# A new order of issue and new engines for the 2587 steps of a fused masked attention and Mish FFN

## The chip, the cores and the metric

The kernel runs on one core of one Trainium2 chip. The time is device microseconds (us) of one execution. TensorE (PE), VectorE (DVE), ScalarE (ACT), GpSimd (POOL) and SyncE (SP, here only an issuer of DMAs) each work through a queue of their own in order; the kernel fixes by hand what stands in each queue, and semaphores tie the queues together.

## The reference

The inputs are q, k and v of shape (4, 8, 768, 64), a projection of 64x6, and two weights of 512x2048 and 2048x512, all float32.

```python
q_bucket = sum((einsum('bhsd,dk->bhsk', q, proj) > 0) * 2**arange(6))   # likewise k_bucket
mask   = q_bucket[:, :, :, None] == k_bucket[:, :, None, :]
scores = where(mask, scale * q @ k.T, -1e9)
attn   = exp(scores - max(scores)); attn = attn / (sum(attn) + 1e-9)
x = (attn @ v).transpose(0, 2, 1, 3).reshape(3072, 512)
h = x @ w_in
g = h * tanh(log1p(exp(h)))          # Mish; for h > 20 the inner function is h itself
out = g @ w_out
```

## The kernel before, in words

Every operand of a product is split into two float16 halves (a high part and the rest), and a product is three float16 matmuls; only the first stretch uses float32 matmuls, because there the halves are not ready.

The work is cut into 12 units (4 batches of 3 units, a unit is 256 query rows of all 8 heads). A unit has 8 score slots of the attention and 8 pieces of the FFN; the FFN of a unit runs three blocks behind its attention. There are 96 score slots in all. The steps of one score slot n, with the lines that a trace shows, are:

- S: the scores on PE into three PSUM banks (L941, or L952 in float32 for the first units), with the bucket bits as a second half of the contraction, so that a masked score is lower by a large constant.
- max on DVE (L982), the reduction over two heads at once; then mb, three tiny operations that make scale and bias of the exponential. It can run on DVE in one piece or column by column (L965 with L969 or L972) or on POOL (L976 and L977).
- exp on ACT (L995, once for each head), which reads the PSUM banks and writes `pb`. From slot 8 on all scores share one PSUM tile (`ps_s`), so S of slot n+1 waits for exp of slot n.
- In unit 0 the exponentials are turned by PE (tp, L424) and copied out of PSUM by ACT (L427) or DVE (L428). In later units they are scaled by the reciprocal of their sum and split: hi (L380 on POOL, L382 on ACT, L383 on DVE) and lo (L398 on DVE, or L404 and L405 on POOL), and a DMA transpose issued by SP turns them (L462, `PT<-hl`).
- V: the product with v on PE (L1092; L1066 in float32 in unit 0, with a spread of the reciprocals, L1076, ahead of it).

The FFN pieces are H (L1120, L1130 to L1132) on PE, Mish on ACT (L1151), a split of the result as above (`ffb`), and O (L1169, L1179 to L1181) on PE, then a copy (L1222 on ACT, L1228 on DVE) and a store (L1232). Exponential and Mish are in two table sets of ACT; the kernel writes a table load (L1340) wherever the next step of ACT needs the other set.

Ahead of the first slots stand the preparation of q and k: float32 turns on PE (L440), a hash on PE (L451) and its threshold on DVE (L454), sums of squares on ACT (L470), a sum over partitions on PE (L488, L489) whose exponent DVE takes (L493, L475), the projection's halves (L513, L514), and for later slots the f16 halves of k (k_hi L383/L380, k_lo L398 or L404 and L405) that SP turns into `KT` (L462, `KT<-wo`). The weights are loaded by SP (L458), unpacked (L586 on ACT, L589 or L593, L599) and split during the first units. Several tiles serve as storage for something else at first: `KT<-wo` is a turn of the halves of k that lie in `wo`, and `stg<-in_moe_w_in` a load of half a piece of w_in into `stg`.

What sets the order is a table. The kernel first only lists its 2587 steps; a step has one to four ways to be done, each on an engine, and `ORDER` is a string of step numbers, each with a letter for the way ("a" is left out). This loop writes the instructions in that order, and each engine meets its own in that order:

```python
for w in ORDER.split():
    n, a = (int(w[:-1]), "abcd".index(w[-1])) if w[-1].isalpha() else (int(w), 0)
    o = self.ops[n]
    assert all(q in done for q in o.preds), o.name
    done.add(o)
    if o.kind and o.kind != table:
        table = o.kind
        load(table)
    yield o.alts[a][2]
```

The ways of mb, as an example of a step with four:

```python
op("mb", [("DVE", 300, lambda: scale(both, False)), ("DVE", 400, lambda: scale(each, False)),
          ("DVE", 500, lambda: scale(each, True)), ("POOL", 600, scale_pool)], ...)
```

Of the kernel before, what the change touches and what calls it, by code (L numbers as in the profile page):

```python
# [86 lines left out]
7 9 0 50 20 22 19 11 12 1 2 3 4 76 29 80 5 77 52 30 13 37 60 25 81b 6 17 26b 38 10 14 15 18 33 34 48 54 57 56 21  # L87
53 39b 63 27 61 35 62 28 31 36 32 78 64 65 16 79 86 82 87 88c 8 137 40 41b 147 83 117 92 94b 138 42 51 43 44 89
109 110b 153 111 90 66 154 112 67 118 119c 120 132 113 115 114 116 124 133 125b 155 126 121 148 46b 91 93b 139b
140b 122 156 107b 123 45 127b 149 134d 23 58 24 59 95 101 135 136 141 55 47 178 96 128 97 99 98 142 84 143 129  # L90
68 100 174 176 175 177 69 170 130 179 171b 168d 108 180 131 172 70 71 204 182 173b 157 189 205b 144b 158 159c
190b 181 193 145b 102 198 191 185 192 186 220 187 206 194 150 199b 85 103 221 161b 195d 160c 197 188 307 222d
258 207 196 216 218 217b 219b 183d 104 223 146 49 152 162 151 106 105 212 213b 163 214 243 210b 215b 184 164 169
211 224 248 239 241 240 353 242 270 235 236 254 255 237 256 244 245b 238 246 233d 249 166b 354 247 262 271 250
200 257 234 259 263b 272d 165b 355 208 251 273 225 292 266 268 267 269 283 293 294 284 349 226 368 357b 350 264
265b 303 285 304b 227 209 305 295 296 201 260d 309d 310 167 356c 306 312b 252 253 203 232 202 291 311c 274 228
281b 261 282 322 286b 317 318 319b 364 287 365 289 288 290 366 313b 323c 308 324 321 320 367 72 330b 369b 231
358 338 315 331 275 325 297 332 276b 298b 229 339 340d 334 230 341 342 397 314 73 333b 74 299 399 336 277 370b
# [12 lines left out]
687 636b 665b 668 639 640c 641 689 619b 680 715b 624 653 716 625b 670c 717 661b 726 679 626 681 727 728d 719 690
720 730 729 718 683 682 732d 691 692c 782 694 662 666 733 721 669 734b 695 778 723 724 741 736 742 775 779 776b
791 696 697 743 792 744 745 765c 735b 693b 672 698 699b 671 777b 766 738 722 737 725 731 795 773 700 637 739 767
768c 769 770 780b 771 772 702 781b 796 703 786 740 704 814 787 815 829 788d 793b 790 789 806d 705 797c 673 706c
708 794 807 808 809 816 817 818 784 810 819 820 799 830 747 709 746 837 811 812 813 821b 822 823c 783 798b 800
801 707 748 749 832 831 710 833 711 713 834c 849 858 750 825b 835 836 826 824c 827 751 712b 752c 754 850 851 761
874 714 828 861 881 762 877 862 863 875 864 852b 854 865 866d 885 853c 763 856 867 868c 870 755 878 756 890 886
855 857 871 882 753 838 894 879 869b 757 880 887c 839 872 785 759 888 889 910 911 883 884 859b 764 895 901c 891
902 903 912 913b 914 905 915 916c 873 909 898 758b 840 842b 760 899 896b 841 892b 904c 1053 907 917 918c 927 900
928 929c 920b 897 956 1174 843 908 906 1012 921 844 960 931 930 933c 942 845 919c 893b 846 922 934 847b 848 935b  # L120
804 802 943 944b 937 924 957 970 926 925 1013 945 958b 946 947c 964 936c 803 939 948 923 938 860 971 949c 1014
1015b 961 950 951 965 940 952 941 932 974 955 966 962 967d 953 1016c 1052 959 1054 969 968 981c 975 982 983 1017
991 992 993 990 805b 985 994 995 996c 954 1018 978 986 876 979 984b 987 963 988 1007 997 972c 973b 980 1008 1009
998 1000 976b 1010 1011 1025c 977 999c 1026 1002b 989 1055 1005 1001 1028 1003 1036 1019 1004 1059 1024 1037
1038 1027c 1029 1039 1040 1041c 1031 1056 1176 1042 1043c 1063 1045 1064 1065c 1020 1030 1032 1046 1044b 1047
1048 1234 1006 1049 1033 1177 1068 1060 1057b 1061c 1067 1066 1079c 1080 1021b 1058b 1089 1082c 1178 1142 1022
1081b 1083b 1062b 1085b 1072 1069 1090 1091c 1092 1093 1094 1095 1073 1076 1105 1096b 1070c 1077 1050 1179b 1074
1098b 1071b 1034b 1106 1107c 1078 1204 1023 1084 1086 1109 1108 1111d 1097c 1100 1075 1112 1113c 1115b 1138 1088
1134 1120 1139 1135 1087 1152 1103 1121 1122c 1099 1101 1116 1124 1123 1125c 1114c 1181 1117 1126 1127c 1129
1128 1136b 1143 1144 1145c 1110 1102 1148 1133 1131 1147 1146 1118 1137 1159d 1130 1169 1104 1132 1175 1156 1182  # L130
1180c 1160 1161c 1153 1149 1170 1171c 1172 1140 1162b 1141b 1163 1173 1188d 1165 1189 1190c 1192 1199 1119 1164
1193 1166 1200 1168 1167 1157 1205 1206 1207b 1158 1191c 1209 1194 1150c 1154c 1151 1197 1196 1183 1201d 1203
1202 1217c 1218 1220b 1219b 1228 1229 1230c 1231 1221 1232 1248d 1263 1259 1267 1264 1260 1261b 1210 1051 1233
1195 1223 1184 1186 1185 1155 1249 1268 1269b 1270 1250b 1252 1271 1287d 1222 1187 1208c 1251c 1254 1235 1236
# [1236 lines left out]
```

## Time and profile before

| | before |
|---|---|
| time, median of 3 runs | 808.07 us (807.68 to 808.2) |
| profiled execution, its own time | 807.16 us |
| its span | 805.4 us |
| PE busy | 796.2 us, 99% of the span, 6595 instructions |
| DVE busy | 620.0 us, 77% |
| ACT busy | 608.7 us, 76% |
| POOL busy | 383.5 us, 48% |
| DMA | 134.30 MB, mean 167 GB/s |
| instruction queue (q8) | 51 packets, 0.84 MB, 0.4% of the DMA engines' span |
| chain that ended last | PE 97%, DVE 1%, DMA 1% |

Between the span and the profiled execution's own time lie 1.76 us. The profiled execution is 0.91 us below the median of the three runs. In the rows further down, each row of a timeline is one instruction or a run of like ones: start in us from the span's start, length in us, engine, line, operation, tiles written and read; in brackets is how long the engine stood idle just before, and what released it.

### The profile page before, as it was taken

How to read it: one execution, taken by the hardware profiler on the slowest of the kernel's cores; microseconds unless marked ns; L12 is line 12 of the kernel's file. 1: busy time of each engine (PE TensorE's matmuls, PEld its weight loads, DVE VectorE, ACT ScalarE, POOL GpSimd, SP SyncE). 2: the span in 40 equal slices, each digit the busy share in tenths (PEclk: the TensorE clock that was granted, in tenths of full speed). 3: DMA queues.
4: the chain of work that ended last, by engine and by line, in shares of the span. 5: the costliest groups of instructions: out<-in, count | busy, mean ns of one | idle time of the engine just before them, and what ended most of it. 6: DMA issues, size and time to landing. Idle time of an engine off the chain costs nothing.

```text
span 805.4 us, 17073 instructions
## 1 busy us (share of the span) xinstructions
PE 796.2 (99%) x6595; PEld 555.0 (69%) x6595; DVE 620.0 (77%) x1139; ACT 608.7 (76%) x930; POOL 383.5 (48%) x398
## 2 busy tenths in 40 slices
PE   9999999999999999999999999999999999999998
PEld 6566666676786676676676776676676677676676
DVE  4888999997898878889798777887887967657200
ACT  5989998998689687677876787898687585778021
POOL 5565442356274293163534245444664771565040
PEclk9999999999999999999999999999999999999999
DMA  9959999989999886999989988999989658455400
GB/s 293 246 168 245 229 215 182 203 179 211 205 178 188 153 170 135 184 192 213 177 139 178 210 140 152 187 171 212 172 162 160 135 91 153 105 99 113 98 2 26
DMA packets 395490, 134.30 MB, mean 167 GB/s; under 512 B 365456, under 2 KB 386448, under 8 KB 395408
## 3 DMA queue, kind: packets, MB, share of 16 engines
q1 hardware_dynamic: 395408, 133.21, 83.1%
q8 instruction: 51, 0.84, 0.4%
q14 instruction: 31, 0.25, 0.1%
HBM read 35.65 MB, written 6.29 MB: 52 GB/s over the span
## 4 chain that ended last, share of the span: by engine, by line
PE 97%; DVE 1%; DMA 1%; ACT 0%; issue 0%; POOL 0%; SPq 0%; DVEq 0%; ACTq 0%
PE ps_s L941 13%; PE ps_t L1092 11%; PE ps_acc L1130 10%; PE ps_acc L1131 10%; PE ps_acc L1132 10%; PE ps_o L1179 9%; PE ps_o L1180 9%; PE ps_o L1181 9%; PE ps_o L1169 4%; PE ps_acc L1120 3%; PE ps_s L952 3%; PE ps_t L1066 1%; PE ps_l L424 1%; PE ps_t L739 1%; DMA stg<-in_v_dram 1%; PE ps_l L354 0%
## 5 line engine op out<-in xcount | busy, mean ns | idle before, releaser
L995 ACT ACTIVATE pb<-ps_s,svb 128x768 f32<-128x768 f32 x184 | 180.9, 987 | 80.1 <-DVE svb L969 29.5
L982 DVE TENSOR_REDUCE svb<-ps_s 128x2 f32<-128x1536 f32 x92 | 161.5, 1755 | 43.6 <-PE ps_s L941 34.2
L1132 PE MATMUL ps_acc<-X,wo 128*128 128x256 f16 x616 | 167.9, 273 | 0.0
L1130 PE MATMUL ps_acc<-X,wo 128*128 128x256 f16 x616 | 167.9, 273 | 0.0
L1131 PE MATMUL ps_acc<-X,wo 128*128 128x256 f16 x616 | 167.9, 273 | 0.0
L398 DVE SCALAR_TENSOR_TENSOR hl<-pb,svb,hl 128x768 f16<-128x768 f32 x137 | 141.0, 1036 | 3.6 <-POOL hl L380 1.5
L1340 ACT ACT_TABLE_LOAD x103 | 132.1, 1283 | 1.8
L1179 PE MATMUL ps_o<-wi,ffb 128*128 128x512 f16 x336 | 127.3, 379 | 0.0
L1181 PE MATMUL ps_o<-wi,ffb 128*128 128x512 f16 x336 | 127.3, 379 | 0.0
L1180 PE MATMUL ps_o<-wi,ffb 128*128 128x512 f16 x336 | 127.3, 379 | 0.0
L941 PE MATMUL ps_s<-KT,QT 128*128 128x512 f16 (+1 forms) x656 | 120.1, 326 | 0.0
L380 POOL TENSOR_SCALAR hl<-pb,svb 128x768 f16<-128x768 f32 x58 | 60.9, 1053 | 77.4 <-DVE svb L1025 39.3
L1092 PE MATMUL ps_t<-PT,VT 128*64 128x256 f16 x1584 | 90.7, 273 | 0.0
L1092 PEld LDWEIGHTS <-VT 128*64 128x64 f16 x1584 | 84.8, 110 | 8.1 <-issue 7.7
L941 PEld LDWEIGHTS <-QT 128*128 128x128 f16 x672 | 63.9, 98 | 37.2 <-issue 5.4
L1151 ACT ACTIVATE ffb<-ps_acc,smalls 128x512 f32<-128x512 f32 x88 | 58.5, 684 | 36.0 <-PE ps_acc L1132 30.9
L404 POOL TENSOR_SCALAR pb<-pb,svb 128x768 f32<-128x768 f32 x39 | 41.5, 1065 | 63.9 <-ACT hl L382 34.2
L1130 PEld LDWEIGHTS <-wo 128*128 128x128 f16 x616 | 60.2, 98 | 12.9 <-issue 0.2
L1131 PEld LDWEIGHTS <-wo 128*128 128x128 f16 x616 | 60.3, 98 | 12.8
L405 POOL TENSOR_TENSOR hl<-pb,hl 128x768 f16<-128x768 f32 x39 | 64.9, 1663 | 3.3
L1132 PEld LDWEIGHTS <-wo 128*128 128x128 f16 x616 | 60.3, 98 | 7.0
L382 ACT ACTIVATE hl<-pb,svb 128x768 f16<-128x768 f32 x57 | 52.6, 930 | 14.7 <-DMA PT<-hl 9.1
(243 smaller groups left out, 1309.4 us busy)
## 6 DMA issues: line engine op xcount, KB each, us to landing
out_dram<-ffb SPq DMA_DIRECT2D x22, 256.0 KB, 3.0
stg<-in_v_dram SPq DMA_DIRECT2D x13, 384.0 KB, 4.1
stg<-in_k_dram SPq DMA_DIRECT2D x12, 384.0 KB, 3.9
wo<-in_q_dram SPq DMA_DIRECT2D x9, 512.0 KB, 5.1
stg<-in_moe_w_in_dram SPq DMA_DIRECT2D x8, 512.0 KB, 4.9
stg<-in_moe_w_out_dram SPq DMA_DIRECT2D x6, 512.0 KB, 4.1
PT<-hl SPq DMA_TRANSPOSE x176, 4.0
wo<-in_moe_w_out_dram SPq DMA_DIRECT2D x5, 512.0 KB, 6.5
```

The costliest lines, as they stand in the source:

```text
L398: return [("DVE", 215 + 1.035 * n, port(lambda: nc.vector.scalar_tensor_tensor(out=dst, in0=src, scalar=sc, in1=hi, op0=ALU.mult, op1=ALU. ...
L941: nc.tensor.matmul(ps[:, hh * S + c0 * P:hh * S + c1 * P], QTb[:, u % 2, sl, qi], KTb[:, j, sl, hh * NCH + c0:hh * NCH + c1].rearrange("p ...
L982: op("max", [("DVE", 1755, lambda: nc.vector.tensor_reduce(out=sv[:, 0], in_=ps.rearrange("p (h e) -> p h e", e=S), axis=AX.X, op=ALU.max, ...
L995: EXP[n, hh] = op("exp", [("ACT", 1075, lambda hh=hh, t=t: nc.scalar.activation(pb[:, t], HOMES[n][0][:, hh * S:(hh + 1) * S], AF.Exp, bia ...
L1092: nc.tensor.matmul(pv[hh * D:(hh + 1) * D, y * 256:(y + 1) * 256], vt[:, w, hh * NCH + c], pt[:, hh, a * NCH + c].rearrange("p s t -> p (s ...
L1130: nc.tensor.matmul(o, wh, X[:, 0, c], start=(c == 0), stop=False)
L1131: nc.tensor.matmul(o, wh, X[:, 1, c], start=False, stop=False)
L1132: nc.tensor.matmul(o, wl, X[:, 0, c], start=False, stop=(c == NCC - 1))
L1179: nc.tensor.matmul(PS[f"o{s}"], gh, wh, start=first, stop=False)
L1180: nc.tensor.matmul(PS[f"o{s}"], gh, wl, start=False, stop=False)
L1181: nc.tensor.matmul(PS[f"o{s}"], gl, wh, start=False, stop=last)
L1340: for fn in plan.ordered("exp", lambda x: nc.scalar.preload_act_table_set(sets[x])):
```

## The change

Only the string `ORDER` is replaced. It has the same 2587 numbers in another order, and 459 of them carry another letter, so they are done in another way, most on another engine. No function, tile or loop is touched. The whole diff is one table of numbers; its first lines are:

```diff
@@ -84,118 +84,118 @@
 ORDER = """
-7 9 0 50 20 22 19 11 12 1 2 3 4 76 29 80 5 77 52 30 13 37 60 25 81b 6 17 26b 38 10 14 15 18 33 34 48 54 57 56 21
...
+50 20 12 11 19 22 5 0 1 2 3 4 7 8 9 80 76 33 29 34b 17 30b 18 6 13 77 81 37 25 14 26 35 27 38 15 52 60 39b 41b
...
```

The order on PE is nearly the same. In all, mb stands on POOL 16 times in place of 22, and ACT's queue has 91 table loads in place of 103. Three places are shown: SP's queue near the start, DVE's queue around the first two score slots, and ACT's queue at the slot with number 5.

SP's queue from the first transposes on; the tile ahead of the arrow is written, and a row with x2 is two DMAs. Before:

```order
L458 DMA stg<-in_moe_w_in_dram 128x2x512
L458 DMA wi<-in_moe_w_in_dram 128x2x512
L458 DMA stg<-in_moe_w_in_dram 128x2x512
L458 DMA wi<-in_moe_w_in_dram 128x2x512
L462 DMA_TRANSPOSE KT<-wo 128x12x128 x2
L458 DMA stg<-in_v_dram 128x2x384
L462 DMA_TRANSPOSE QT<-tok_65 128x8x128
L462 DMA_TRANSPOSE KT<-wo 128x12x128 x2
L458 DMA X<-in_q_dram 128x8x128
```

The same stretch of the changed kernel:

```order
L458 DMA wi<-in_moe_w_in_dram 128x2x512
L462 DMA_TRANSPOSE KT<-wo 128x12x128 x2
L458 DMA stg<-in_v_dram 128x2x384
L458 DMA stg<-in_moe_w_in_dram 128x2x512
L458 DMA wi<-in_moe_w_in_dram 128x2x512
L462 DMA_TRANSPOSE QT<-tok_65 128x8x128
L462 DMA_TRANSPOSE KT<-wo 128x12x128
L458 DMA X<-in_q_dram 128x8x128
L458 DMA stg<-in_moe_w_in_dram 128x2x512
L458 DMA wo<-in_moe_w_in_dram 128x2x512
L462 DMA_TRANSPOSE KT<-wo 128x12x128
```

The four loads of w_in stood ahead of the first pair of `KT` transposes; now one does, two stand behind that pair, and the second half of the piece in `stg` stands behind the third `KT` transpose.

DVE's queue around the first two score slots (L982 on `ps_s` is the maximum of slot 0, on `ps_b` that of slot 1). Before:

```order
L493 TENSOR_SCALAR smalls<-ps_t 128x1
L475 TENSOR_SCALAR smalls<-smalls 128x1
L513 TENSOR_SCALAR pj<-pj_80,smalls 128x6
L514 SCALAR_TENSOR_TENSOR pj<-pj_80,smalls,pj 128x6
L454 TENSOR_SCALAR KT<-ps_l,smalls 128x384
L982 TENSOR_REDUCE svb<-ps_s 128x2
L965 TENSOR_SCALAR svb<-svb,smalls 128x1 x2
L969 TENSOR_SCALAR svb<-svb 128x1 x2
L454 TENSOR_SCALAR KT<-ps_t,smalls 128x384
L743 TENSOR_REDUCE hsum<-ps_t 128x48
L428 COPY PT<-ps_l 128x3x128
L982 TENSOR_REDUCE svb<-ps_b 128x2
```

The changed kernel:

```order
L454 TENSOR_SCALAR KT<-ps_t,smalls 128x384
L454 TENSOR_SCALAR KT<-ps_l,smalls 128x384
L493 TENSOR_SCALAR smalls<-ps_t 128x1
L475 TENSOR_SCALAR smalls<-smalls 128x1
L383 TENSOR_SCALAR wo<-PT,smalls 128x12x64
L982 TENSOR_REDUCE svb<-ps_s 128x2
L965 TENSOR_SCALAR svb<-svb,smalls 128x2
L972 TENSOR_TENSOR svb<-svb 128x2
L454 TENSOR_SCALAR KT<-ps_t,smalls 128x384
L743 TENSOR_REDUCE hsum<-ps_t 128x48
L398 SCALAR_TENSOR_TENSOR wo<-PT,smalls,wo 128x12x64
L982 TENSOR_REDUCE svb<-ps_b 128x2
```

The high and low halves of k (L383, L398 on `wo`) that POOL made before (L380, L404 and L405) are now made by DVE, one ahead of each maximum; the copy L428 has gone from ahead of the second maximum to behind it; and the pair L513 and L514 now stands further up, ahead of the hash thresholds of q and k (L454) on which slot 0 waits.

ACT's queue at slot 5 (L995 on `ps_s`; L586, L593 and L470 on `wi`, `wo` or `stg` are unpacking of weights). Before:

```order
L586 ACTIVATE wi<-wi 128x1024
L427 COPY PT<-ps_t 128x3x128
L427 COPY PT<-ps_l 128x3x128
L470 ACTIVATE wo,smalls<-wo 128x1024
L593 ACTIVATE wi<-wi 128x1024
L995 ACTIVATE pb,svb<-ps_s,svb 128x768
```

The changed kernel:

```order
L586 ACTIVATE wi<-wi 128x1024
L427 COPY PT<-ps_l 128x3x128
L427 COPY PT<-ps_t 128x3x128
L586 ACTIVATE stg<-stg 128x1024
L995 ACTIVATE pb,svb<-ps_s,svb 128x768
```

The operation L586 on `stg`, which needs both halves of the w_in piece in `stg` and stood 16 rows further up, now stands directly ahead of the exponential.

## Rows read from the trace of the kernel before

**Rows 1.** Busy time by stretch (stretch, length, busy us of each engine, granted clock, DMA)

```profile
0.00:72.00 72.00, 66.56 (x556) 44.54 (x557) 55.12 (x132) 57.50 (x111) 43.02 (x56) 1.00 0.87 236
72.00:802.00 730.00, 729.55 (x6040) 510.49 (x6039) 564.43 (x1007) 551.20 (x820) 340.46 (x343) 1.00 0.84 160
802.00:805.40 3.40, 0.07 (x1) 0.00 (x0) 0.48 (x1) 0.00 (x0) 0.00 (x0) 0.89 0.23 77
```

**Rows 2.** Waits of PE (waiting, releaser; us in total, times, longest)

```profile
PE ps_l L424 <- DVE PT L428: 1.1, 3, 0.5
PE ps_l L354 <- DVE floors L348: 1.0, 1, 1.0
PE ps_t L1066 <- ACT PT L427: 0.6, 1, 0.6
PE ps_l L424 <- ACT PT L427: 0.5, 2, 0.2
PE ps_t L1076 <- DVE smalls L493: 0.3, 1, 0.3
...
PE ps_t L488 <- ACT PT L427: 0.2, 1, 0.2
```

**Rows 3.** Timeline of PE, 32 to 34 us and the end of one score round

```profile
32.04 0.55 PE L424 MATMUL ps_l<-ffb,pb 128*128 128x128 f32 x3 [0.47 <-DVE PT L428]
32.77 0.19 PE L488 MATMUL ps_t<-smalls,ones 128*128 128x2 bf16 x2 [0.18 <-ACT PT L427]
...
33.30 0.66 PE L1076 MATMUL ps_t<-ffb,svb 128*64 128x128 f32 x8 [0.33 <-DVE smalls L493]
...
206.98 0.81 PE L941 MATMUL ps_s<-KT,QT 128*128 128x512 f16 x4
```

**Rows 4.** Timeline of SP's queue, two places

```profile
17.00 8.62 SPq L462 DMA_TRANSPOSE KT<-wo  x2
...
29.27 4.91 SPq L462 DMA_TRANSPOSE KT<-wo  x2
```

**Rows 5.** Timeline of POOL, two places

```profile
22.54 1.64 POOL L405 TENSOR_TENSOR wo<-PT,wo 128x768 f16<-128x768 f32 x1
...
37.80 1.31 POOL L976 TENSOR_SCALAR svb<-svb,smalls 128x2 f32<-128x2 f32 x1 [0.48 <-DVE smalls L910]
```

**Rows 6.** Timeline of DVE ahead of slot 0

```profile
13.30 0.30 DVE L513 TENSOR_SCALAR pj<-pj,smalls 128x6 f16<-128x6 f32 x1
13.63 0.23 DVE L514 SCALAR_TENSOR_TENSOR pj<-pj,smalls,pj 128x6 f16<-128x6 f32 x1
```

**Rows 7.** Three lines of the kernel (count, duration ns min/median/max, first and last start)

```profile
L398 DVE SCALAR_TENSOR_TENSOR hl<-pb,svb,hl x137: 993/1015/1650, 69.6 to 745.6; 128x768 f16<-128x768 f32 x137
...
L976 POOL TENSOR_SCALAR svb<-svb,smalls x22: 297/856/2233, 24.9 to 713.5; 128x2 f32<-128x2 f32 x22
...
L1340 ACT ACT_TABLE_LOAD  x103: 1283/1283/1283, 77.6 to 742.8; - x103
```

**Rows 8.** Timeline of ACT, at slot 5, in one round, and at one table load

```profile
35.19 1.15 ACT L586 ACTIVATE wi<-wi 128x1024 f32<-128x1024 f32 x1
...
39.42 0.99 ACT L995 ACTIVATE pb<-ps_s,svb 128x768 f32<-128x768 f32 x1 [0.19 <-POOL svb L977]
...
205.10 0.99 ACT L995 ACTIVATE pb<-ps_s,svb 128x768 f32<-128x768 f32 x1
...
444.88 1.28 ACT L1340 ACT_TABLE_LOAD   x1
446.18 0.99 ACT L995 ACTIVATE pb<-ps_s,svb 128x768 f32<-128x768 f32 x1
```

**Rows 9.** DMA issues (KB each, median us from issue to landing)

```profile
stg<-in_moe_w_in_dram SPq DMA_DIRECT2D x8, 512.0 KB, 4.9
...
ext<-in_v_dram SPq DMA_DIRECT2D x3, 384.0 KB, 8.4
```

**Rows 10.** Landing of the transposes that SP issues for PT

```profile
DMA to landing us min/median/max: 3.6/4.0/7.3
```

More of the change, by code (lines that the diff above doesn't have):

```diff
@@ new lines @@
+168d 144b 129 174 176 157 175 177 179 158 180d 100 170 130 171 131 172 70 71 182 150 181 183c 198 145 173b 204
+189 193 159 161 205b 190b 194 191 185 186 192 208 199 169 184 49 23 101 152 146 162 151 220 187 206 84 195c 221
+207 197 188 216 218 196 160b 307 217b 219b 222d 102 212 223 213 163 214 200 85 164 103 243 353 244 224 215 241
+239 104 106 105 240 248 245d 242b 270 235 236 254 237 233c 255 247 246 166b 249 354 271 238b 250 368c 256 251
+225 262 292 260d 165 210 258 226 272b 257 211 528 355c 273 263b 293 209b 266 268 267 269 283 284b 234 349 201
@@ new lines @@
+350 264 265b 303 285 261 304b 274 294d 295 305 296 259 227 309c 357 310 253 281b 282 286b 317 167 203 356c 252
+202 232 228 322 323b 231 312c 306 311b 313b 291 318 319c 364 287 365 289 288 290 366 320 321 324 315 330 72 367
+331 358 314 325 328 316 338 229 339 332b 369b 230 334 340 397 73 399 297 275 276b 298b 342 341 370c 299 333c
+423c 74 398 400 300 371 277 336 278 378 351 421 422 372b 374b 335 329 302 301 379 380 424 352 381 382 373 389
+359 337 375 280 279 308 360 404 425 376b 409 383 390 410b 405 427 326 456 449 391c 393 392 384b 406d 408 407
@@ new lines @@
+515 525 499 520 553 540 552 568b 569 570 544 545 546 572 501 500 502 526 503b 585 586 587 539 541 504 527 543
+583 588 505 506 576 547 571c 574 507 589 607 590c 577b 591 578 592c 594b 608 609c 554 613 575 573 555 582 598
+584 556 557 650 599 646 558 559 643 561 610 560 611 627d 642 644 628 593 629 612 562 647 651 579c 580 631 596
+645 648 600 654 563 564 655 659 614 615 616 565 656c 617 618c 620 657 658 601 649 566 595 630 604 635 674d 675
+633 632 597 676c 678b 621 684 663 602b 603 660 685 622 623 634 701 567 774 667 686d 652b 638b 639 640c 641 689
@@ new lines @@
+664 677 688 636 653 619c 625 624 626 679 687 605b 715 716 726 680 717c 727 681 668 661b 670b 690 691 692b 728c
+662 783 694 718c 719b 730 729 732 782 721 720 665b 666 733 734c 736b 695 683 778 775 724 682 741 723 742 669
+743c 791 696 776b 779 735 722 737 731 725 773 693c 744 745 703 765c 697 698b 699 700 738 777 780b 671b 704 795
+766 767 705 672c 781 769 792 793c 768 796 786 787 788c 673 771b 739 606 702 770 772 837 740 814 815 829 797 706
+789 790 708 806c 798 807 816 808b 809b 817 818c 707 819 810 820 821c 799 800 794 812 822 823c 825b 830 637 746
@@ new lines @@
+709 747 811 813 801 748 749 832 849 710 831 833 834 711 713 750 761 712 826 874 858 836 835 859 850c 824c 827
+751 752c 754 851 861 714 828 877 762 881 862 863 852b 853b 864 854 785 784 865 866d 763 856 885 867 868c 753c
+870 755 855 857 878 890 756 882 838 894 886 869c 887b 872 839 875b 879b 888 889 901c 757 759 880 911 871 902 764
+904c 895 891 912 913 903c 905 914 915 873 909 898 910 840 758b 842b 760 916d 883c 907 884 1052 964 841 899 917
+804b 1012 843 860 927 928 900 929 906 908 924 956 844 892 802 918 920 1053 919c 960 921 1013 896b 1014 845 930
@@ new lines @@
+1032 1175 1046 1020 1044 1047 1066 1067 1049 1033 1034 1079c 1048 1054 1061 1062 1080 1022 1068 1057b 1050 1089
+1177 1081b 1178 1021b 1058b 1035 1023 1082 1179b 1090 1091c 1092 1083 1093 1072 1076 1105 1073 1085 1094 1095
+1096b 1098b 1084 1074c 1075b 1097b 1100b 1106 1069 1107c 1070b 1108 1109 1077 1180 1138 1134 1111b 1112 1071
+1099 1086 1113b 1101 1204 1120 1121 1088 1087 1122b 1114c 1115 1135 1139 1152 1103 1117 1123 1124 1125b 1126
+1136c 1143 1144 1145 1116 1128 1131 1110 1102 1148 1146 1181 1118 1234 1127b 1137 1078 1129b 1147 1159c 1160
@@ new lines @@
+1161c 1163b 1130 1162c 1169 1170 1171c 1132 1133 1104 1156 1149 1172 1173 1165 1233 1182 1164 1188c 1140b 1189
+1190b 1141b 1192 1199 1205 1206 1200 1193 1051 1166 1157 1150 1119 1168 1167 1201d 1158 1191c 1207 1183 1184
+1383 1194 1209 1197 1195 1203 1202 1217d 1228 1229 1218 1186 1153 1154b 1185 1230c 1231 1219c 1221 1220 1232
+1248c 1223 1151b 1249 1250b 1252b 1259 1216 1263 1210 1267 1222 1268 1269 1155 1264 1260 1261b 1251b 1254 1211
+1276 1196 1256 1187 1224 1270 1271 1287d 1262 1297 1208b 1212 1288 1289 1291b 1214 1213 1298 1299 1253 1272 1235
@@ new lines @@
+1236 1237 1198 1290 1301 1300 1238 1239b 1255 1280 1273 1316b 1317 1241 1318b 1320b 1265 1215 1293 1327 1328
+1329 1257b 1285b 1274b 1281 1277 1283b 1330 1302 1292 1319c 1240c 1322 1266 1275b 1225 1375 1331 1379 1376 1380
+1278 1333d 1334 1226b 1294 1321 1335b 1337b 1242 1323 1227 1338 1342 1282 1343 1344c 1296 1286 1336b 1345 1346
+1366c 1367 1304 1368 1339 1295 1396 1243 1387 1348 1244 1377 1340 1258 1369 1325 1305 1392 1332 1324 1388 1389b
+1279 1306 1372 1390 1307b 1370b 1391 1378 1245 1284 1407b 1408 1384 1246 1309 1417 1326 1374 1371 1410b 1381
@@ new lines @@
+1418 1382 1419c 1393 1409c 1397 1373 1411 1420 1421 1422d 1400 1401 1394c 1413 1423 1402 1347 1247 1308b 1310
+1303 1412 1414 1433 1341 1311 1415 1424 1349 1350 1434 1312 1426b 1435b 1478 1351 1314b 1425b 1398b 1399 1313
+1315 1427 1438 1436 1437 1451d 1395 1352 1428 1462 1463 1452 1353b 1355 1405 1464d 1453c 1455 1482 1483 1479
+1466 1465 1430 1416 1454c 1385 1491 1356 1429 1456 1486 1431 1357 1432 1403c 1354c 1480c 1481 1467b 1468 1457
+1458 1439 1495 1450 1440 1487 1488b 1441 1469b 1358 1470c 1471 1404 1489 1490 1502c 1473 1362 1443 1503 1360b
@@ new lines @@
+1359b 1512 1472 1361 1513 1504c 1514 1505b 1444 1474 1775 1506 1496 1459 1561 1363 1475 1364 1515 1516 1442c
+1508 1365 1386 1445 1613 1517 1460 1492 1565 1518 1446 1447 1493c 1528 1448b 1519 1529 1484c 1494 1485 1653 1497
+1530d 1476b 1531 1499 1500 1614 1510 1461 1449 1507 1509 1521 1532 1557 1534b 1535 1498 1520 1523 1615 1616 1511
+1543 1558 1562 1536b 1544 1545 1538 1743 1559c 1560 1522 1524 1539 1546 1547 1548c 1537c 1549 1654 1525 1526
+1575 1540b 1576 1566 1551 1550 1567 1501 1554 1568 1406 1571 1527 1533 1542 1556 1541 1555 1572 1552 1553 1569
@@ new lines @@
+1655 1573c 1617b 1618 1570 1582c 1583 1585 1592 1593 1594 1584b 1563 1564 1595 1586 1574 1596 1597b 1588 1598
+1619 1477 1591 1579 1835 1587 1589 1608 1599 1777 1580 1577c 1609 1610c 1611 1600c 1581 1601b 1602 1612 1626
+1627 1629 1628b 1603 1604 1590 1606 1605 1625 1620 1637 1660 1638 1630 1639c 1578b 1632 1607 1656 1640 1641 1664
+1621 1622b 1642d 1643 1644b 1646b 1631 1634 1778 1650 1805 1633 1647 1661 1673 1657 1645b 1665 1666c 1779 1648
+1668 1667 1635 1658b 1680 1681 1649 1690 1682b 1684 1691 1692c 1693 1669 1683c 1686 1651b 1694 1677 1695b 1659b
@@ new lines @@
+1876b 1905 1931 1932 1934d 1896 1926 1976 1906 1943 1895 1922 1884c 1920c 1885 1847 1935 1923b 1907 1944 1945c
+1936 1937 1908b 1940 1879c 1910 1946 1938b 1947 1967d 1886b 1887 1968 1904 1848 1924 1925 1980 1927 1988 1933
+1977 1939 1911 1949 1948 1981 1969 1909 1880b 1989 1978c 1971 1990c 1991 1992 1970b 1973 1950 2008c 1951 1993
+1941 1942 1975 1912 1997 1913 1952 2018 1859 1972 2009 1979 1914 2010b 1998 2011 2017 2012 1953 1915 1994 1954
+1982c 1999 1974 2001 2039 1916 1828 2013 2019 1986 2020c 2014 1956 1983b 2015 1957 2021 2022 2023c 1963 2024
@@ new lines @@
+1987 2025b 2027b 2002 2003 2034 2000b 1955 1995b 2006b 2035 2036c 2038 2037 2052b 2026 2029b 1996 2053 2054 2040
+2016 2032 2083 1964 2063 2079 2031 2064 2065b 2028 2041 2055c 2066 2056b 2067 2068d 2030 2057 2051 2069 2033
+2087 2076 2060 2058b 2042b 2044 2088 2089 1965 2084 2070 2080 2071b 2045 2059 2090 2072 2091 2074 2081c 2103b
+2082 2096 1958 1959 1960b 2104 2113 2114 2166 2105b 1961b 2097 2077 2061 2092 2046 2111 2047 2107b 2093 2098b
+2075 2073 1962 2214 2100 2085c 2115b 2116 2106 2117 2086 2043b 2007 1966 2118c 2129 2119 2048 2130 2120 2101
@@ new lines @@
+2327c 2328 2329c 2304 2342b 2330 2331 2253 2320 2332 2338 2333b 2339b 2343b 2312 2354 2345 2306 2335 2350 2346
+2347c 2348 2349 2361c 2280 2371 2321 2351 2362 2363c 2365 2364 2352b 2355 2372 2373c 2374 2375 2376c 2367b 2334
+2358 2359 2370 2360 2356c 2387 2353 2377 2388 2389b 2378b 2390 2380 2391 2393c 2394 2368 2357b 2395b 2397 2366
+2379 2381 2398 2385 2420 2369 2424 2384 2421 2404 2422c 2382 2383 2423b 2405 2406 2407 2408 2409d 2396b 2386
+2392 2433 2434 2425 2399b 2428 2417 2437 2499 2401 2429 2430d 2431 2410 2411 2412b 2415 2413 2432 2438 2444c
@@ L199 @@
+2543 2525 2547 2538 2546 2539 2554 2540c 2548 2549 2544 2541b 2558 2559 2560c 2561 2526 2529 2550 2551 2545b
+2555 2552 2562 2563 2564 2565b 2556c 2557 2570 2553 2566 2567 2568b 2572 2571 2569 2574 2573 2576 2579 2575 2582
+2581 2577b 2580 2578 2585b 2586 2583b 2584
 """
```

149 lines of the change are left out of this document (38 added, 111 removed).

## The prediction

> **What bounds the kernel now.** I read the busy time by stretch first [rows 1]. The reader is to see two numbers: between 72 and 802 us PE is busy 729.55 of 730.00 us, so 0.45 us is all that any order can win there; in the first 72 us it is busy 66.56, so 5.44 us are open. The last 3.40 us hold one copy on DVE (0.48) and the landing of the last store. The granted clock is 1.00 in both long stretches, the upper of its two levels (2.4 GHz), and nothing here can raise it. PE's own list of waits comes next [rows 2]: all of its entries lie in the first 72 us, its five largest sum to 3.5 us, three more of 0.2 (one is shown) bring 4.1, and 1.0 of that is the start, where PE waits for a first constant. So 3.1 us is what a better order could take from PE as far as the trace names a releaser. The rest of the 5.44 is the time before PE's first instruction and short gaps without one.
>
> Then the timelines of the queues in that stretch, to see what is late. SP is held 8.62 us by a pair of transposes from 17.00 on [rows 4]; POOL ends the low half of k that the second of them needs at 22.54 + 1.64 = 24.18 [rows 5]. Behind that pair stand in SP's queue the load of v and all that follows. Around 32 to 33.3 us PE then waits three times: 0.47, 0.18 and 0.33 [rows 3], together 0.98.
>
> **The change part by part.** The PE work is the same: same products, nearly the same order. So the sum is made of PE's waits alone, against the profiled execution (807.16).
>
> *Start.* The pair L513 and L514 (from 13.30 to 13.63 + 0.23 = 13.86 us, 0.56 [rows 6]) now runs ahead of the thresholds on which slot 0 waits. Bounds: 0, if DVE is waiting for the hash products there anyway, and 0.56; I take 0.3, the middle.
>
> *Halves of k on DVE.* The low half (L398) stands ahead of slot 1's maximum. The trace shows no L398 on this tile; the same form takes 1.02 us on another [rows 7]. The copy L428 that stood there has gone behind the maximum, which gives some of it back. Slots 1 to 3 are chained by maximum, exponential and turn, so what is late here stays late until slot 3. Bounds: 0 (the copy and idle time cover it) and 1.02; I take 0.25. With the start, slot 3 is 0.55 late.
>
> *SP's queue.* With both halves of k made ahead of slot 1's maximum and not at 24.18, the pair of transposes no longer holds SP until 25.62, and the load of v, the sums behind it and the spread L1076 come earlier than PE wants them. The three waits of 0.98 [rows 3] go. Bounds: 0 and 0.98; I take all of it, since their releasers all hang on that load or on a copy that has moved from behind a maximum on DVE to ACT.
>
> *mb off POOL.* For slot 5 mb took 1.31 us on POOL [rows 5], and the exponential started 0.19 after ACT was free, at 39.42 [rows 8]. It goes to DVE. PE is then in the product V of unit 0 and does not wait, so this is worth its share of the other 3.1 - 0.98 = 2.1 us of waits: bounds 0 and 2.1. I take 0.2, because the order still shows the copies for which PE waits (L428) standing behind a maximum on DVE in the same places.
>
> *Steady state.* About 400 more steps change engine or place. They hide behind PE as long as each S finds its exponential done. A tight round: the second exponential ends at 205.10 + 0.99 = 206.09 [rows 8], the next S starts at 206.98 [rows 3], a margin of 0.9. A mb on POOL takes 0.30, 0.86 or 2.23 us (least, median, most) [rows 7]; at the median it fits in the margin beside what it takes on DVE, at the most it costs PE about 1.3 once. There are 16 of them now, not 22, and few in tight rounds. Bounds: a gain of 0.45 [rows 1], a loss of 1.3 for each bad meeting; I take 0.
>
> *Transfers reckoned late.* The transposes for V land in 3.6, 4.0 and 7.3 us (least, median, most) [rows 10], and the list of waits has no V that waits for one [rows 2]. Moving them earlier gains nothing; it costs only if hi and lo, hurried, delay a maximum. I take 0.
>
> *Table loads.* Twelve fewer at 1.283 us [rows 7] free 15.4 us of ACT. The exponential behind one starts 1.30 after it (444.88 to 446.18) [rows 8], so nothing else is paid. ACT is busy 551.20 of 730 us [rows 1] and PE does not wait for it there: worth 0, and at most the 0.45. The Trainium skill, "ScalarE: Activation LUTs", section "What ACT_TABLE_LOAD costs", states about 1.28 us for the load and another 1.38 for a drain, 2.66 for a switch; by it 12 switches would be 32 us of ACT, an estimate. The trace agrees with the load and shows no drain; by either price the sum stays, because PE is the bound.
>
> *End.* The last copies move from ACT to DVE; the very last was on DVE before (0.48) [rows 1]. Worth 0, at worst 0.48.
>
> The sum: 807.16 + 0.55 - 0.98 - 0.2 = 806.53, that is 0.63 below. The median of the runs is 0.91 above the profiled execution, so on its basis 808.07 - 0.63, about 807.4.
>
> **The rivals.** A measurement of this kernel can tell about 0.2%, 1.6 us, from no change.
>
> *No change worth the name* (my forecast, with the case that the waits merely move): between 806.5 and 809.6 us. For it speaks that 0.45 us are open after 72 us. It includes that the change doesn't do what it says: no wait for a late transfer stands in the list, so a plan that guards against them has nothing to win. Chance 0.61.
>
> *Faster.* The whole 3.1 us of named waits goes, slots 0 to 3 pay nothing, and with the 0.45 that would be 808.07 - 3.55 = 804.5; half of it, 1.6 and more, is needed. For it: the new order attacks just this stretch. Against: 0.55 is paid first, and two thirds of the rest hang on copies that stand where they stood. Likely time 805.9. Chance 0.17.
>
> *A weight load that comes late (slower).* ACT's L586 on the second `stg` load now stands directly ahead of slot 5's exponential, 16 rows later than before, but its load has gone behind the third `KT` transpose in SP's queue. Its issue lies between 31.2 (right after the first transpose from 29.27 on) and 34.8 (if SP stays held to 29.27 + 4.91 = 34.18 as before, and one more load) [rows 4]; I take 32. Landing: 4.9 us by the median of such loads, 8.4 by the slowest group [rows 9], so between 36.1 and 43.2, by my values 36.9. Slot 5's exponential started at 39.42, and an L586 of this size takes 1.15 [rows 8], so from about 38.3 on each us of delay is a us on the exponential, then on the turns of slot 5, for which PE has no other work in its queue. It decides from about 40.5 (0.6 to eat up the gain, 1.6 beyond it). At a landing of 41.5 the loss is 3.2: 808.07 + 3.2 - 0.6 = 810.7. Against it: my value lies 1.4 us ahead of the point where it costs anything. Chance 0.12.
>
> *New waits in tight rounds (slower).* Two bad meetings of mb on POOL, or of hi placed between a maximum and mb, at 1.3 each: 808.07 - 0.6 + 2.6 = 810.1. For it: 459 steps moved and the margin is 0.9. Against: the kernel before had 22 such chances, and the 730 us show 0.45. Chance 0.10.
>
> **How the numbers follow.** The predicted time is that of the likeliest, 807.4. The range leaves out about one in ten on each side: from 805.6, which keeps most of the faster case, to 810.3, which takes in tight rounds and half of the weight load. Faster 0.17; slower 0.12 + 0.10, less a little for small cases, 0.21; same 0.62.
>
> **What would show it.** Right: PE still busy 729.5 or so of the 730 us before the tail; the waits at 32 to 33.3 gone from PE's list; SP's first pair of transposes short, under 4 us in place of 8.62; L976 16 times, table loads 91 with the same 1283 ns; slot 3's S later than before and H of unit 0 earlier, both by about half a us. Wrong on the fast side: no wait above 0.2 left in PE's list but the first. Wrong on the slow side: ACT idle ahead of L586 on `stg` at 37 to 41 us, released by a DMA; or S (L941) after 100 us in PE's list of waits, released by L995. A tail longer than 3.5 us would show that the end was not free.

## The result, and the profile after

The changed kernel takes 814.73 us (median of 4 runs, 813.22 to 815.23), the kernel before 807.88 beside it: a ratio of 1.0082, 95% interval 1.0065 to 1.0099. It is slower by 6.9 us, and by more than the range allowed (up to 810.3). The profiled execution has a span of 812.5 us, 7.1 more than before. The kernel before, run 60 times more beside the kernels further down, took 807.82 us (median) in the 39 runs with a granted clock of 0.999 or 1.0 and 810.15 in the 21 with 0.996 to 0.998.

First the busy time by stretch, read as [rows 1]:

```profile
0.00:72.00 72.00, 65.76 (x555) 43.58 (x556) 56.29 (x135) 57.58 (x113) 34.96 (x50) 1.00 0.85 232
72.00:802.00 730.00, 725.06 (x5990) 505.25 (x5989) 556.17 (x1020) 538.81 (x811) 334.84 (x327) 1.00 0.83 160
802.00:812.50 10.50, 7.18 (x55) 5.04 (x52) 1.88 (x4) 0.47 (x1) 0.00 (x0) 1.00 0.15 50
```

Between 72 and 802 us PE is now idle 4.94 us where it was idle 0.45. DVE, ACT and POOL are all less busy than before in that stretch (556 against 564, 539 against 551, 335 against 340), so no engine became a bound: PE waits although the others have more time left. Over the whole span PE's busy time is also 1.8 us longer (798.0 against 796.2) for the same 6595 instructions, so idle time alone does not show the whole loss. What PE waits for is in its list; the two largest lines that are new against [rows 2] are:

```profile
PE ps_s L941 <- ACT pb L995: 2.1, 4, 0.9
PE ps_t L488 <- ACT tok L470: 1.1, 1, 1.1
```

The first is the score S waiting for the exponential of the slot before it. The list names only the longer gaps. To find the others I subtracted the start of the same score in the two traces; where the difference grows, time is lost. Only slots are shown whose score stands behind as much work on PE in both orders; at others the difference jumps by up to 3 us and back, because the score has more or fewer products ahead of it:

| score of slot | start before, us | start after, us | difference, us |
|---|---|---|---|
| 4 | 34.42 | 34.24 | -0.18 |
| 16 | 117.06 | 117.79 | 0.73 |
| 21 | 162.77 | 164.01 | 1.24 |
| 27 | 213.81 | 216.54 | 2.73 |
| 30 | 235.28 | 239.14 | 3.86 |
| 54 | 415.40 | 420.32 | 4.92 |
| 56 | 432.61 | 438.55 | 5.94 |
| 86 | 663.03 | 669.62 | 6.59 |
| 95 | 736.49 | 743.61 | 7.12 |

The loss is not in one place. It comes in steps of 0.1 to 1.5 us, each at a slot or two, and nothing but 0.2 us behind slot 56 is won back between them.

The longest single wait of a score in the list is at slot 30. DVE and POOL there, then PE:

```profile
231.77 2.50 DVE L383 TENSOR_SCALAR hl<-pb,svb 128x768 f16<-128x768 f32 x1
234.18 1.75 DVE L982 TENSOR_REDUCE svb<-ps_s 128x2 f32<-128x1536 f32 x1
```

```profile
230.31 1.33 POOL L404 TENSOR_SCALAR wo<-wo,smalls 128x1024 f32<-128x1024 f32 x1
231.72 2.13 POOL L405 TENSOR_TENSOR tok<-wo,tok 128x1024 f16<-128x1024 f32 x1
```

```profile
239.14 1.03 PE L941 MATMUL ps_s<-KT,QT 128*128 128x512 f16 x6 [0.88 <-ACT pb L995]
```

L383 of this size takes 0.62 us (its median in this trace); here it takes 2.50, and it ends 0.42 after POOL's subtraction, 231.72 + 2.13 = 233.85. The maximum stands behind it, so the exponential and slot 30's score come late. In the kernel before the same two operations run on the same two engines, but the maximum is first:

```profile
230.03 1.76 DVE L982 TENSOR_REDUCE svb<-ps_s 128x2 f32<-128x1536 f32 x1
...
233.21 0.61 DVE L383 TENSOR_SCALAR hl<-pb,svb 128x768 f16<-128x768 f32 x1
```

```profile
229.62 2.13 POOL L405 TENSOR_TENSOR tok<-wo,tok 128x1024 f16<-128x1024 f32 x1
```

There POOL's subtraction runs beside the maximum, which takes its usual 1.76, and ends at 231.75; L383 comes after both.

### The profile page after: what moved, and what is told of

The parts are those of the page before. It is cut to its first block, busy times and chain, and to the rows that moved or that the text cites. A ratio compares the mean times of both kernels' runs of the same rounds, so it can differ in the third digit from the quotient of the medians.

```text
span 812.5 us, 17047 instructions
## 1 busy us (share of the span) xinstructions
PE 798.0 (98%) x6595; PEld 553.9 (68%) x6595; DVE 614.3 (76%) x1157; ACT 596.9 (73%) x924; POOL 369.8 (46%) x376
## 5 line engine op out<-in xcount | busy, mean ns | idle before, releaser
L995 ACT ACTIVATE pb<-ps_s,svb 128x768 f32<-128x768 f32 x184 | 180.9, 986 | 103.0 <-DVE svb L972 42.7
L982 DVE TENSOR_REDUCE svb<-ps_s 128x2 f32<-128x1536 f32 x92 | 161.3, 1753 | 35.4 <-PE ps_s L941 27.7
L398 DVE SCALAR_TENSOR_TENSOR hl<-pb,svb,hl 128x768 f16<-128x768 f32 x129 | 140.3, 1091 | 11.0 <-POOL hl L380 5.4
L941 PE MATMUL ps_s<-KT,QT 128*128 128x512 f16 (+1 forms) x656 | 120.1, 326 | 2.5 <-ACT pb L995 2.1
L1340 ACT ACT_TABLE_LOAD x91 | 116.8, 1283 | 1.6
L380 POOL TENSOR_SCALAR hl<-pb,svb 128x768 f16<-128x768 f32 x60 | 62.1, 1037 | 119.8 <-DVE svb L1025 92.7
L941 PEld LDWEIGHTS <-QT 128*128 128x128 f16 x672 | 63.6, 98 | 39.3 <-issue 8.8
L404 POOL TENSOR_SCALAR pb<-pb,svb 128x768 f32<-128x768 f32 x47 | 46.8, 996 | 90.9 <-ACT hl L382 45.6
L405 POOL TENSOR_TENSOR hl<-pb,hl 128x768 f16<-128x768 f32 x47 | 80.1, 1704 | 3.9
L382 ACT ACTIVATE hl<-pb,svb 128x768 f16<-128x768 f32 x60 | 55.4, 929 | 25.0 <-DMA PT<-hl 15.8
```

What stands on the lines that cost most here:

```text
L398: return [("DVE", 215 + 1.035 * n, port(lambda: nc.vector.scalar_tensor_tensor(out=dst, in0=src, scalar=sc, in1=hi, op0=ALU.mult, op1=ALU. ...
L941: nc.tensor.matmul(ps[:, hh * S + c0 * P:hh * S + c1 * P], QTb[:, u % 2, sl, qi], KTb[:, j, sl, hh * NCH + c0:hh * NCH + c1].rearrange("p ...
L982: op("max", [("DVE", 1755, lambda: nc.vector.tensor_reduce(out=sv[:, 0], in_=ps.rearrange("p (h e) -> p h e", e=S), axis=AX.X, op=ALU.max, ...
L995: EXP[n, hh] = op("exp", [("ACT", 1075, lambda hh=hh, t=t: nc.scalar.activation(pb[:, t], HOMES[n][0][:, hh * S:(hh + 1) * S], AF.Exp, bia ...
L1340: for fn in plan.ordered("exp", lambda x: nc.scalar.preload_act_table_set(sets[x])):
```

## The experiments

**Which part of the order.** From any slot on, the steps that are left can follow the other table, since each table keeps every step behind those it needs. Two kernels take one table up to the score of slot 16 and the other from there:

```
before:        ORDER = old table up to the score of slot 16, then the rest in the old order
front new:     ORDER = new table up to the score of slot 16, then the rest in the old order
rest new:      ORDER = old table up to the score of slot 16, then the rest in the new order
```

> The new order up to the score of slot 16 (about 117 us), the old order from there. If the loss is made in the first stretch and only carried on, this has all of it, about 814.5 us. If the loss is made round by round after that (my theory, from the difference of PE's starts: 0.7 us lost by slot 16, 7.1 by slot 95), this takes about 808.6 us, 0.7 above the old order.

> The old order up to the score of slot 16, the new order from there: the counterpart. Round by round: about 814.2 us (6.4 above the old order). First stretch: about 808.

The first took 808.54 us, ratio 0.9999 (0.9988 to 1.0010); the second 814.74, ratio 1.0076 (1.0056 to 1.0096). The ratio of the first is flattered by its company: all of its runs had a granted clock of 0.999 or 1.0, and 10 of the 27 of the kernel before beside it had less. Against the other 17 (807.68) the new start costs 0.9 us, near the 0.7 expected; the loss is made after slot 16, but for that part.

**Two stretches put into the old order.** The kernel is the old order with the new one between two scores only:

```
ORDER = old table up to the score of slot 24 (28), new table up to slot 28 (32), then the rest in the old order
```

> The old order, with the new order for the steps between the scores of slots 24 and 28 alone. Theory of late transfers: in the new order a k load and a k transpose stand later in SP's queue there, the square of the loaded keys ends late, and PE's small sum (L488) waits for it; so this stretch alone costs 1.0 to 1.5 us (about 809.2) and shows PE waiting for L470 on ACT. Theory that the engines' stretched operations alone cost the time: nothing here, 807.9.

> The old order, with the new order for the steps between the scores of slots 28 and 32 alone. Theory of stretched operations: the high half on DVE (L383) stands ahead of slot 29's maximum and takes 2.5 us in place of 0.62 while POOL subtracts (L405, 2.13 us); the maximum and the exponential come 1.9 us late and slot 30's score waits about 0.9; this stretch alone costs about 1.1 us (809.0). Theory of late transfers alone: 807.9.

The first took 811.95, ratio 1.0035 (1.0020 to 1.0049), but it is a miss as a test: PE waits 2.1 us for L470, and that wait lies at the seam ahead of slot 24, where steps that the old order has later now come at once, not ahead of slot 27, where the new order waits. The second took 811.97, ratio 1.0037 (1.0022 to 1.0051), three times the loss expected. The timelines of DVE and POOL there show the step of slot 30 again, from the same operation:

```profile
230.57 2.49 DVE L383 TENSOR_SCALAR hl<-pb,svb 128x768 f16<-128x768 f32 x1
232.99 1.75 DVE L982 TENSOR_REDUCE svb<-ps_s 128x2 f32<-128x1536 f32 x1
```

```profile
230.53 2.13 POOL L405 TENSOR_TENSOR tok<-wo,tok 128x1024 f16<-128x1024 f32 x1
```

Slots 29 and 30 lose 1.5 us together there, 0.70 of it in PE's wait for the exponential. The rest is elsewhere: 1.27 between slots 30 and 33 at the other seam, and 1.15 in the first 25 us, which are the old order's own and differ from one execution to another (0.2 in the trace of the graft before it). So a seam costs as much as what it is to test, and I went over to single edits of the new table.

**Order against engines.**

```diff
-904c 895 891 912 913 903c 905 914 915 873 909 898 910 840 758b 842b 760 916d 883c 907 884 1052 964 841 899 917
+904c 895 891 912 913b 903 905 914 915 873 909 898 910 840 758b 842b 760 916c 883 907 884 1052 964 841 899 917
...
```

These are one line of the first (the numbers as in the new order, every letter as in the old) out of the 459 changes; the second has the numbers as in the old order and every letter as in the new.

> The new order with the old letters, so every step on the engine that it had before. If the order of the queues makes the loss, this loses at least as much as the new kernel, 814.7 or more; if the choice of engines makes it, this is near 808. I expect 818, more than the new kernel, because the order was laid out for other engines.

> The old order with the new letters: the counterpart. If the choice of engines makes the loss (more low halves on POOL, 47 against 39, next to more work on DVE), this takes 814 or more; if the order does, near 808. I expect 816, for the same reason: neither half fits the other, and the two would then not tell the shares.

They took 928.89 and 924.90 us, 14% more, and PE waits all through for the exponentials; the first line of PE's list of waits of the first:

```profile
PE ps_s L941 <- ACT pb L995: 53.4, 33, 5.5
```

I had expected 818 and 816. As foreseen they don't divide the loss between order and engines, but they show how little room a round has: with 459 letters that don't fit their places, 120 us are lost. (In the first some 30 of them are PE's own: it is busy 826.1 us in place of 796.2, at a granted clock of 0.974.)

**One letter: is it the stretched operation?**

```diff
-904c 895 891 912 913 903c 905 914 915 873 909 898 910 840 758b 842b 760 916d
+904 895 891 912 913 903c 905 914 915 873 909 898 910 840 758b 842b 760 916d     # a1: the high half on ACT
+904c 895 891 912 913 903c 905 914 915 873 909 898 910 840 758b 842 760 916d     # a5: POOL's low half of q on DVE
```

> The new order with one letter changed: the high half that DVE made in 2.50 us ahead of slot 29's maximum is made by ACT. If the stretched operation made slot 30's score wait (0.88 us, released by the exponential), that wait is gone here or under 0.2, and slot 30's score comes about 1 us earlier against the scores before it. If DVE were simply full there, a wait of 0.3 or more stays, since only 0.6 us of DVE's usual work is taken away.

> The new order with one letter changed, another one: the high half stays on DVE ahead of slot 29's maximum, but the low half of q that POOL made beside it (L404 and L405, 2.13 us for the subtraction) goes to DVE, two operations behind that maximum. If POOL's subtraction held DVE up, L383 takes 0.6 us there, the maximum starts about 1.9 us earlier and slot 30's wait of 0.88 goes, though DVE now has more work. If the high half ahead of the maximum is late for another reason, it still takes about 2.5 us.

> The new order with the high half of slot 28 on ACT, timed. The one stretched operation cost 1.1 us in the trace: about 813.6. Its single run before was at 811.0; if that holds, the one letter gives back more than its own wait, because what comes after runs earlier against its transfers.

In a1 slot 30 waits no longer. A single run took 810.96; timed it took 812.49, ratio 1.0057 (1.0043 to 1.0072), against 1.0082 of the new order, so this one letter gives back about 2 us, one more than the wait it removes. In its trace slot 27 also lost 0.5 in place of 1.5, though its steps are the same; why is not shown. In a5 (one run, 813.19) the high half stays on DVE ahead of the maximum, and takes its usual time as soon as POOL does nothing beside it (DVE's timeline of a5):

```profile
229.49 0.61 DVE L383 TENSOR_SCALAR hl<-pb,svb 128x768 f16<-128x768 f32 x1
230.04 1.76 DVE L982 TENSOR_REDUCE svb<-ps_s 128x2 f32<-128x1536 f32 x1
```

Slot 30 loses nothing there, though DVE has 1.28 us more to do; that work then costs about 2.0 us by slot 32. So it was POOL's subtraction that held DVE, and not the amount of DVE's work.

**Transfers moved forward at slot 27.** Four steps of SP's queue, in the new table:

```diff
-... 739 606 702 770 772 837 740 ...        708 806c ...        637 746
-709 747 811 813
+... 739 606 702 747 770 772 740 ...        708 709 746 837 806c ...        637
+811 813
```

> The new order with four steps moved in SP's queue alone: one k or v load goes ahead of two transposes, and the transpose of k and a load go ahead of a load of q and a store. If PE's wait of 1.09 at L488 (at 213.9) came from transfers issued late, L470 on ACT starts about 3 us earlier and the wait is gone. If ACT or PE's own place for L488 made it, a wait of about 1 us stays. The time of either of these two looks is about 813.7, one us below the new order, within what single runs scatter.

One run took 816.46, more than the new order. The wait at L488 is gone, but others stand in its place in PE's list:

```profile
PE ps_s L941 <- ACT pb L995: 3.3, 6, 1.4
PE ps_t L1092 <- DMA PT<-hl: 1.2, 1, 1.2
```

The product V now waits for a transpose, a wait that neither kernel had. Here, what went forward in SP's queue put back another transfer that was as urgent.

**Several places mended.**

```diff
-451 452c 453 ... 457 443b 486 459 460d 433 461
+451 452c 453 ... 457 443b 486 459 460b 433 461
-645 648 600 654 563 564 655 659 614
+645 648 600 654 655 659 563 564 614
-904c 895
+904 895
-974 941 955 966 967d 969
+974 941 955 966 967b 969
-2441 2449 2447c 2450 2451 2464 2442 2470 2468 2467 2507
-2471 2472c 2443
+2441 2449 2447c 2464 2442 2470 2468 2467 2507
+2471 2472c 2450 2451 2443
```

> The new order with five places mended: the letter of a1, two mb from POOL to DVE (slots 15 and 33), the sum behind a transpose of k (L739 at 157.5) one product later on PE, and a low half (L398, 2.27 us beside POOL) behind slot 95's maximum. If the loss is a sum of such places, each worth 0.2 to 0.6 us, this takes 1.3 to 1.8 us less than a1. If it is not local, but the order lacks room everywhere, each mended place opens another, and it takes as long as a1.

It took 811.96, ratio 1.0048 (1.0032 to 1.0063): 0.7 us less than a1 by the ratios, half of what was expected and within the intervals. (The expectation counts three slots one too high; the edits are as shown.) The step at slot 16 is gone, where in the new order mb of slot 14 had run on POOL in two pieces of 1.1 us (POOL's timeline of the new order):

```profile
106.00 1.09 POOL L976 TENSOR_SCALAR svb<-svb,smalls 128x2 f32<-128x2 f32 x1
107.17 1.08 POOL L977 TENSOR_TENSOR svb<-svb 128x2 f32<-128x2 f32 x1
```

The step at slot 95 is not: it is 0.5 with the low half behind the maximum as with it ahead. Behind the maximum the low half, which reads `pb`, holds the exponential itself (ACT's timeline of a6):

```profile
738.97 0.99 ACT L995 ACTIVATE pb<-ps_s,svb 128x768 f32<-128x768 f32 x1 [4.09 <-DVE hl L398]
```

Nor is the step at slot 21: PE no longer waits for the transpose of k there, but 0.41 for a sum on DVE (L743), and the slot loses 0.48 in place of 0.40. So of the five edits two bought nothing. And in this execution slot 27 lost 0.99 and slot 56 lost 1.63, both steps that hang on transfers.

**A transpose of q behind those for V, at slot 56.** What the new order does there, in the timelines of SP's queue, of ACT and of PE:

```profile
422.23 4.59 SPq L462 DMA_TRANSPOSE QT<-tok  x1
426.90 11.75 SPq L462 DMA_TRANSPOSE PT<-hl  x5
```

```profile
431.62 0.94 ACT L382 ACTIVATE hl<-pb,svb 128x768 f16<-128x768 f32 x1 [1.63 <-DMA PT<-hl]
```

```profile
438.55 1.46 PE L941 MATMUL ps_s<-KT,QT 128*128 128x512 f16 x8 [0.59 <-ACT pb L995]
```

The high half on ACT may only be written when the transpose that reads its buffer has landed; ACT waits 1.63 us for it, DVE's low half and the next maximum (433.83) stand behind, and the score waits.

```diff
-1530d 1476b 1531 1499 1500 1614 1510 1461 1449 1507 1509 1521
+1530d 1476b 1531 1499 1500 1614 1510 1461 1507 1509 1449 1521
```

> The kernel of a6 with one more edit: in SP's queue the transpose of q ahead of slot 56 (4.59 us on the queue, landed 7.9 us after its issue) goes behind the two transposes for V that followed it, as in the old order. If the late landing of the first of those two (431.5, for which ACT's L382, then DVE's L398 and the maximum of slot 56 waited) made slot 56's score about 1 us late, the loss between slots 55 and 56 falls from 0.9 to 1.6 us to 0.3 or less, and the time to about 811.0. If the transposes land as late wherever they stand, the loss stays near 1.

SP's queue in it, from the same place on:

```profile
421.39 4.40 SPq L462 DMA_TRANSPOSE PT<-hl  x2
425.90 3.02 SPq L462 DMA_TRANSPOSE QT<-tok  x1
```

It took 810.59, ratio 1.0013 (1.0003 to 1.0024). Between slots 54 and 56 under 0.2 us is lost, where six traces of the new order's steps there lost 0.9 to 1.6 and a seventh (a1) 0.2. By the ratios the gain from a6 would be 0.35% or 2.8 us, but the kernel before took 809.07 beside a7 and 807.70 beside a6. By the medians of the two kernels themselves it is 1.4 us, which that step covers. Against the 8 runs of the kernel before beside a7 with a granted clock of 0.999 or 1.0 (808.43), as all runs of a7 had, a7 is 2.2 us slower: with six places of 2587 changed, about two thirds of the 6.9 us are gone. It doesn't beat the kernel before.

## Why the prediction was wrong, by its own steps

**What bounds the kernel: right.** PE is the bound in both, and the headroom of 0.45 us after 72 us was the whole of what could be won there. That said nothing on what could be lost.

**The start and the halves of k: right in kind, too dear.** I took 0.3 and 0.25. The score of slot 0 came 0.10 later and the maximum of slot 1 at 19.72, no later than before (19.76): L398 took 1.01 there and stood where idle time and the moved copy had been.

**SP's queue: partly.** The pair of transposes held SP less, but not under 4 us as I wrote (SP's timeline after the change):

```profile
16.98 5.51 SPq L462 DMA_TRANSPOSE KT<-wo  x2
...
29.75 1.47 SPq L462 DMA_TRANSPOSE KT<-wo  x1
31.27 0.96 SPq L458 DMA_DIRECT2D X<-in_q_dram  x1
32.28 0.64 SPq L458 DMA_DIRECT2D stg<-in_moe_w_in_dram  x1
```

Of the three waits of [rows 3], worth 0.98, only that for DVE's copy went; 0.16 and 0.33 stayed, and waits of 0.22 and 0.29 came beside them. Slot 4 came 0.18 earlier (0.43 in my sum), slot 6 0.3 earlier (0.1 more, where mb had left POOL; 0.2 in my sum), and by slot 9, at 62 us, 0.6 was given back, with one new wait of 0.51 for a copy on DVE at 54.63. By slot 10 the trace is 0.33 late, and the new start alone costs 0.9 us in the first experiment: a small loss, not the gain of 0.63.

**The weight load: the rival did not come about.** The load was issued at 32.28 (I took 32) and landed at 37.7 (I took 36.9). ACT's timeline there:

```profile
37.72 1.14 ACT L586 ACTIVATE stg<-stg 128x1024 f32<-128x1024 f32 x1
38.76 0.97 ACT L995 ACTIVATE pb<-ps_s,svb 128x768 f32<-128x768 f32 x1
```

L586 starts as the load lands, and the exponential at 38.76 is earlier than the 39.42 of [rows 8].

**Table loads and end: right.** 91 loads of 1283 ns in place of 103, worth nothing to the time. The stretch behind the last matmul is 3.3 us in both.

**The steady state: the step that failed.** I took 0 with a loss of 1.3 for each bad meeting, "few in tight rounds". Of the 7.1 us, 6.8 were lost behind slot 10, and the sign that I had named for the slow side, S (L941) waiting for L995 after 100 us, is there. Three things were wrong in the step. I priced the meetings by mb on POOL alone [rows 7], by L976, which is only the first of its two operations there (1.09 + 1.08 at slot 14), and took the least and the most of L976 as its own scatter. The same meetings stretch DVE's halves: L383 from 0.62 to 2.50, and at slot 94 L398 from 1.01 to 2.27, both ahead of a maximum; that the second cost anything is not shown (see a6). The row above L976 in [rows 7] already had an L398 of 1.65. I counted the letters that changed and did not look in the order for what had gone ahead of a maximum; at slot 29 the order shows it, L383 behind L982 before and ahead of it after, with POOL's subtraction on the same engine in both. And the rival that names this ("new waits in tight rounds", with hi between a maximum and mb) was held to two meetings at 1.3 and a chance of 0.10, since the trace of before shows 0.45 us lost in 22 chances. That the old order lost nothing was a property of that order, not of the rounds: at slot 29 it kept the meeting beside the maximum, where it cost nothing.

**Transfers: the other step that failed.** I wrote that reckoning them late "costs only if hi and lo, hurried, delay a maximum", and took 0. At slot 56 just this happened, by way of the buffer of the high half, for 1.0 us, and a7 points to the cause: with one transpose moved in SP's queue the step is gone (in one trace, and a1 without that edit lost only 0.2 there). At slot 27 PE waited for a small sum of squares whose keys came late (timelines of SP's queue and of PE after the change):

```profile
203.26 3.27 SPq L462 DMA_TRANSPOSE KT<-tok  x1
```

```profile
213.90 0.16 PE L488 MATMUL ps_t<-smalls,ones 128*128 128x2 bf16 x1 [1.09 <-ACT tok L470]
```

Before, this transpose stood behind two loads, was issued at 200.21 and landed 4.5 us later; here it stands behind two loads and a store, holds the queue for 3.27 us and lands at 211.0, 7.7 us after its issue. At slot 21 PE waited 0.31 for another (L739). The list of waits of before has none for a transfer, and I read that as proof that transfers don't matter; it only said that they were in time by that order.

**What stays open.** The edits account for the steps at slots 16, 30 and 56, about 2.5 of the 7.1 us in the trace; that at slots 32 and 33 (0.6) went with a1. The others, at slots 21, 27, 54, 77, 86 and 95, about 3.5 us, have no edit that removes them. The step at slot 27 was 1.5 us in the trace of the new order and 0.25 to 0.99 in six others with the same steps there; a2 moved the transfers and lost more. Why it differs between executions is not known.

## What to carry to other kernels

In a kernel whose bound engine idles 0.06% of a stretch, a new order has next to nothing to win there, and the list of waits of the old one prices nothing: ask for each round what now stands ahead of its critical operation, and what that takes at its longest row, not at its median. (Even that is no bound: the longest L383 of this size before took 1.55 us, not 2.50. How much of POOL's operation is still to run prices it better, as the next section shows.) Put the operation that is not held up (here the maximum, which reads PSUM) beside the other engine's long one, and the operation that is held up behind it. A transfer queue that is served in order is a part of the schedule like an engine: what is put ahead of an urgent transpose can reach the bound engine (1.0 us at slot 56).

## What the runs showed of the hardware that I had not expected

An operation of DVE on SBUF tiles can wait out a whole subtraction of POOL: 2.50 and 2.49 us for L383 in two kernels, ending 0.42 and 0.40 after POOL's L405 of 2.13, and 0.61 when POOL was idle. It is not these two alone: in the traces before and after, all 13 rows of L383 of this size that began with more than 0.4 us of one of POOL's long operations (L380, L404, L405) still to run ended 0.41 to 0.42 us after it, 5 of them before the change, 0.90 to 1.55 us long. So the cost could have been read from the trace before. The maximum, which reads PSUM, was never held so: 1.73 to 1.76 us in all 92 of its rows on `ps_s` after the change, though over half of the maxima began beside an operation of POOL. The Trainium skill, "SBUF — State Buffer", section "SBUF: two separate sides", says that DVE, for an operation in a 2-port mode or with two SBUF inputs, and GpSimd share a pair of ports as an exclusive lock: whichever starts first has it for the whole instruction while the other fully blocks. The traces agree with this for L383, which started 0.05 and 0.04 us after L405; in which mode it runs no run shows.

Transposes for V with a packet of the instruction queue within 3.9 us behind their issue landed in 4.8 us (median of 44) after the change, the other 132 in 3.9; before the change 4.9 (35) and 3.9 (141). I worked these out from the times of the packets and landings in the two traces. The late transposes of k and q at slots 27 and 56 named above were both in flight with such a packet (at 208.4 and at 427.9). That fetches made them late was not tried, since no edit here moves a fetch alone.
